# A gated sum of a state-space scan and linear attention: the scan over every sixteenth token instead of every eighth, with a step list drawn up anew

## The chip, the cores and the metric

The kernel runs on one core of one Trainium2 chip. Its five engines work side by side: TensorE (PE in the profile; its weight loads are shown as PEld), VectorE (DVE), ScalarE (ACT), GpSimd (POOL) and SyncE (SP), which here only issues DMAs. The metric is the device time of the slowest core in microseconds; there is only one core. A time is the median of several runs.

## The reference

For x of 2048 tokens and 512 channels (bf16) the output is g * a + (1 - g) * b, with a gate g for each token. Part a is a diagonal complex state-space recurrence with 512 states, part b a linear attention with 32 heads of 16 channels.

```python
g = sigmoid((x * gate_w).sum(-1, keepdims=True))

# a
Lam_bar = exp(dt * Lam)                          # Lam complex, dt = exp(log_dt)
B_bar = ((Lam_bar - 1.0) / Lam)[:, None] * Bmat
Bu = einsum("bld,pd->blp", x + 0j, B_bar)
for t in range(L):
    h = Lam_bar[None, :] * h + Bu[:, t, :]       # hs collects h
a = 2.0 * einsum("blp,dp->bld", hseq, Cmat).real + x * Dskip

# b
phi_q = concat(softmax(q @ w_phi), softmax(-(q @ w_phi)))    # 32 features a head
phi_k = the same of k
kv, z = sum_s phi_k v, sum_s phi_k
b = (phi_q @ kv) / (phi_q @ z + 1e-6) @ wo
```

## The kernel before

**Tokens in residues.** The 2048 tokens are split by their residue r modulo NR = 8. For each r there are NC = 256 columns, two tiles of 128 tokens (index `ti` = 2r + a); the tile pairs lie one after another in `xT`, the transposed x, so that one matmul takes all 256 columns of a residue. Before, column a*128 + c of residue r is token (a*128 + c)*8 + r: a is the half of the sequence. Each x tile is a transposing DMA from HBM (`x_load`), each output tile a DMA into `out_par`.

**The recurrence.** The state dimension is held in eight tiles t of 64 states, real and imaginary part stacked to 128 rows; j = 0 to 3 names a pair of them. Step `g{r}{j}` computes the input products for residue r (eight matmuls of 256 columns against the transposed B, `BT`). For odd r an odd step adds earlier residues: matmuls with `dg`, block-diagonal matrices of the powers 1, 2, 4 and 6 of the decay, against the copies `uv`. So `g7j` ends with the sum of a block of eight tokens, weighted by the decay, for each of 256 blocks, and copies it to `va`, real and imaginary parts separated: four copies of 64 x 256. Step `z{j}` turns this complex recurrence over the 256 blocks into a real one: it multiplies by cosines and sines (`T2c`, `T2s`, tables made by the steps `i{j}` from an iota, two multiplications and two Sin on ScalarE), runs two VectorE scans of length 256 with the decay's eighth power `r8_`, and turns back. The result is the state at the last token of each block, `H7`. The steps `h{r}{j}` then compute the states of residues 0 to 6: a matmul with `dg` against H7 shifted by one block (r = 0, 1, 3, 5), or against the state of r - 1 (r = 2, 4, 6), plus `uv`.

**The rest.** `W`, `f`, `w` fold w_phi into the key and query weights (`W` transposes, `f` and `w` multiply and copy). `k` and `v` are the key and value products of a token tile, `q` the query products; `x`, `n`, `e`, `s` (and for the last groups `X`, `N`, `E`, `S`) are maximum, minimum, exponential and sum of the features, `a` accumulates the key-value matrix. `c` scales C. `y` computes the output products of the recurrence for a token tile, `o` the attention (two matmul groups `pn`, a logarithm, a copy, an exponential, a product, then a transpose by DMA or, for the last four, on TensorE), `t` multiplies with wo into the same PSUM bank, scales by the gate and stores. `M` (on POOL) makes the powers of the decay, `D` (on DVE) spreads them into `dg`. `l`, `N`, `R`, `Q`, `C`, `J`, `O` issue loads on SP: x tiles 8 to 15, the two halves of B (`NI`, `NR`), the transposes of B, of the query weights and of C, copies of the transposed C, and wo.

**What sets the order.** The engines' order is written out by hand, in the string `ORDER` of 865 steps. Each name is a generator that runs up to its next `yield`; the main loop at the end of the function takes the names one by one. A name stands once for each of its yields: `g70 g70` is its matmuls, then the odd step. `@b` gives the PSUM banks that a step may take, `:D` puts a step's PSUM copy or scaling on DVE instead of ScalarE, `:A` issues a store from ScalarE's queue, and `F:n` is n filler matmuls of 128 columns. Each engine takes its instructions strictly in this order. SP too: it runs ahead of the other engines until one of its DMAs has to wait, and what stands behind it waits as well. Ahead of the list SP loads x tiles 0 to 3, the value weights and x tiles 4 to 7.

Of the kernel before, what the change touches and what calls it, by code (L numbers as in the profile page):

```python
# [20 lines left out]
P = 128  # L21
# [13 lines left out]
q0@4 q2 z1 z0 h50@3 z1 z1 g42@7 q0 z1 z1 v10@26 h50 xA z1 h10@0 e4 e4 z1 g42 nA s4 g32@4 v10 g32 a3 g52@3 g32 h60@7 c2
xA s4 c4 O g52 xA c4 R6 z1 z1 v9@26 s4 h10 g52 nA g72@4 g72 c4 h60 v9 a3 J3 g03@3 v11@26 c2 c2 s4 g72 g72 c0 c0 nA
g63@0 z2 z2 v12@74 a3 nA v11 a3 xA g03 z2 z2 z2 z2 xA nA s4 J3 g63 g23@2 c5 s4 v12 g23 h51@6 g13@3 g13 g13 z2 z2 c0 z2
z2 eA g43@0 g43 eA v14@74 v14 J1 h51 s4 g33@2 g33 h52@3 g33 h12@0 g53@6 eA g53 g53 h12 h11@7 h11 h52 eA sA g73@4 g73
g73 g73 v13@26 v13 q10@0 z3 c6 z3 c5 sA z3 z3 v15@73 z3 a4 a4 a4 v15 z3 q10 q5@4 a4 Y z3 h31@0 q5 sA h30@4 z3 q9@2 h31
q13@6 h31 q9 h33@0 h61@7 Y q13 h30 sA sA c5 h62@3 z3 z3 h30 h61 sA Y Y h22@5 q4@2 h62 q4 h33 q15@6 q11@7 h22 h20@4 h20  # L40
h32@2 h32 sA sA c1 q11 h13@1 h13 h32 q14@3 h40@5 h33 c3 h53@7 h42@4 sA h42 h53 c1 c1 sA h21@2 c3 h21 q6@0 q6 q15 c6
q7@1 h63@4 h63 q8@7 h03@0 c3 q7 c6 h40 sA c7 h41@6 h41 y6@2 c7 h03 h03 h43@4 h43 y2@1 h02@5 c7 sA h23@6 h23 h01@0
h00@4 END q8 G X1 y6 y6 q14 y2 N1 X1 h00 h00 N1 y2 h02 h02 X1 N1 G h01 o0@6 y0@7 o0 o0@3 h01 o2@4 o2 X1 o2@5 o2 o2 N1
y5@6 o0 y3@0 X1 N1 y5 X2 o0 o1@4 E1 o2 y0 o2 o0 E1 E1 E1 X2 y1@5 y1 y3 y3 o1 G N2 X2 N2 X2 o0 N2 X2 o3@3 o3 o3@4 S1 o3
o3 G S1 N2 S1 t2 o3 S1 o3 t2 t2:A q12@3 q12 N2 S1 S1 o1@4 o1 o1 o1 o1 S1 S1 E2 S1 y0 y4@1 y9@3 y8@4 y8 y8 X3 E2 E2 S1
S1 S1 N3 X3 E2 t3 X3 X3 X3 S2 N3 t0 t0 t0:A S2 t3 S2 y1 t1 t1 y5 y9 y9 o4@7 o4 o4@0 o4 y4 o4 o4 o4 o5@5 o5 o5@7 o5 o5
y13@0 S2 S2 o6@5 o6 o6@7 o6 o6 y13 N3 y7@5 y7 N3 y7 y13 o5 S2 S2 N3 E3 o5 o6 o6 S2 S2 E3 E3 o7@7 o7:D y4 t4 t4:D t5
o7@7 S2 S2 E3 S3 t5 S2 S3 S3 o7 o7 o7 t6 y11@1 y11 o7 t6 o8@6 o8 o8@7 o8 o8 S3 S3 o8 y12@2 o9@6 o9 o9@7 o8 y11 y12 y12
y10@6 o9 o9 o9 o11@7 o11 o9 S3 S3 y10 y10 o11@7 t7 o11 o11 t7 t8 S3 S3 o11 o11 S3 t8 S3@7 S3:D S3@5 S3 t9 t9 t1:A
o10@4 y15@7 o10:D o10@5 o10:D t8 o10 o10 o10 y15 o12@4 o12:D o12@3 t4 o14@5 o12 o12 o12 t5 o14 t11 o14@4 o14:D o14 o14  # L50
t11 y14@3 t9:A o13@5 o13 o12@4 o12:D y14 o13@1 o13 o13 o15@4 o15:D o15@5 o15 o15 t12 t3:A t10 o13 o13@1 o15 t6:A t11
o14@4 o13:D t7 t10 t10 y15 t12 t12 o15@5 o15 y14 o14:D t13 t14 t14 t14 t13 t13 t15 t15 t15:A
# [18 lines left out]
def kernel(  # L71
# [27 lines left out]
    NC = S // NR  # L99
    NT2 = Pst // 64  # L100
# [7 lines left out]
    out_par = out2.rearrange("(a c r) d -> c r a d", r=NR, c=P)  # L108
# [85 lines left out]
    H7 = pR.tile([P, NT2, ZP + NC], BF16, name="H7")  # L194
# [7 lines left out]
    dg = pBC.tile([P, 4, NT2, P], BF16, name="dg")  # L202
# [18 lines left out]
    T2c = pAC.tile([P, PT, NC], BF16, name="T2c")  # L221
    T2s = pAC.tile([P, PT, NC], BF16, name="T2s")
    uv = [pAC.tile([P, 7, 2, NC], BF16, name=f"uv{j}") for j in range(PT)]
    va = [pAC.tile([P, 2, NC], BF16, name=f"va{j}") for j in range(PT)]
# [4 lines left out]
    x_res = x2.rearrange("(a c r) d -> r a c d", r=NR, c=P)  # L229
# [20 lines left out]
    iot = tabp.tile([P, NC], F32, name="iot", bufs=1)  # L250
    nc.gpsimd.iota(iot[:], pattern=[[1, NC]], base=0, channel_multiplier=0, allow_small_or_imprecise_dtypes=True)
# [15 lines left out]
    dt_, r_, om_, t0, t1, t2, den_, r2_, r4_, om8, r8_ = (par[:, 10 + k, :] for k in range(11))  # L267
# [102 lines left out]
    def st_P4():  # L370
        VS(out=om8, in0=t0, scalar1=float(NR), scalar2=None, op0=ALU.mult)
# [10 lines left out]
    def st_M():  # L382
# [24 lines left out]
        GT(out=dl[:, 9, :], in0=tb[:, 0, :], in1=den_, op=ALU.mult)  # L407
        GT(out=dl[:, 8, :], in0=tb[:, 1, :], in1=den_, op=ALU.mult)
        lo = dl[:, 0:10, :].rearrange("p (k t) j -> p k t j", t=2)
        up = dl[:, 10:20, :].rearrange("p (k t) j -> p k t j", t=2)  # L410
        GS(out=up[:, 0:4, 0], in0=lo[:, 0:4, 1], scalar1=-1.0, scalar2=None, op0=ALU.mult)
        GC(out=up[:, 0:4, 1], in_=lo[:, 0:4, 0])
        GS(out=up[:, 4, 0], in0=lo[:, 4, 0], scalar1=-1.0, scalar2=None, op0=ALU.mult)
        GC(out=up[:, 4, 1], in_=lo[:, 4, 1])
        for h in range(2):
            for ri in range(2):
                GC(out=dgB[ri * 64:(ri + 1) * 64, :, :, h], in_=dl[h * 64:(h + 1) * 64, 10 * ri:10 * ri + 10, :])
        yield

    def st_D():  # L420
# [189 lines left out]
    def st_g(r, j):  # L610
# [12 lines left out]
        if r < 7:  # L623
            evac(uv[j][:, r], pg[:])
            yield
            return
# [238 lines left out]
```

## Time and profile before

| what | value |
|---|---|
| three runs | 156.17, 156.59 and 157.39 us; median 156.59 us |
| the profiled execution | span 153.7 us; 2.9 us below the median of the runs |
| granted TensorE clock | 0.995 mean over the span |
| DMA | 17.03 MB in 48737 packets, mean 111 GB/s |
| HBM | read 2.64 MB, written 2.10 MB |

The span reaches from the first to the last instruction of the program in one profiled execution. The time of a run also has what lies around the span, so the difference of 2.9 us stays in the sum as it is. An engine's busy time counts matmuls, loads of weights and elementwise instructions; a DMA issue, a wait or a branch is not busy time. Matmuls are pipelined, their recorded ends are modelled, and a few matmul records are missing from the trace, so counts of matmuls are taken from the loops of the kernel. A row of the groups reads: line, engine, operation, written tile <- read tiles, shape and type out and in, count | busy us in all, mean ns of one | idle time of the engine just before them, and what ended it.

### The profile page before, as it was taken

To read this page: it belongs to the slowest core of one execution; us is meant where nothing else is said; L and a number is where in the kernel's file an instruction comes from. 1 tells how busy PE (TensorE), PEld (TensorE's weight loads), DVE (VectorE), ACT (ScalarE), POOL (GpSimd) and SP (SyncE) were. 2 spreads that over 40 slices of the span, in tenths; PEclk is the share of its full clock that TensorE was granted. 3 is DMA by queue.
4 is the path that set the end of the run, shared out by engine and by line. 5 is a ranking of instruction groups with operands and counts; after the bars stand their busy time and mean duration, and the time that the engine had idled before them with its cause. 6 is when DMAs were issued, how large, how long until landed. Compare 5 with 4: busy or idle time off the path is not lost.

```text
span 153.7 us, 3412 instructions
## 1 busy us (share of the span) xinstructions
PE 145.5 (95%) x1238; PEld 99.7 (65%) x1254; DVE 131.0 (85%) x302; ACT 136.7 (89%) x322; POOL 12.9 (8%) x43
## 2 busy tenths in 40 slices
PE   7799999999999999999999999999999899999990
PEld 7656665886899858889876565554545455555550
DVE  3599999999999999999999999999999858445510
ACT  3599999999999999999999999999798897577672
POOL 8258800000000000000000000000000000000000
PEclk9999999999999999999999999999999999999998
DMA  4788995544474379960000006603139938667633
GB/s 117 162 220 121 213 171 102 102 86 92 101 102 100 80 146 205 237 133 0 2 4 2 0 0 134 125 18 68 33 82 118 215 80 194 141 118 172 211 123 102
DMA packets 48737, 17.03 MB, mean 111 GB/s; under 512 B 42064, under 2 KB 48720, under 8 KB 48720
## 3 DMA queue, kind: packets, MB, share of 16 engines
q1 hardware_dynamic: 47008, 15.36, 50.6%
q10 hardware_dynamic: 1552, 1.44, 2.9%
q8 instruction: 10, 0.16, 0.5%
q0 software_dynamic: 160, 0.01, 0.2%
q14 instruction: 7, 0.06, 0.1%
HBM read 2.64 MB, written 2.10 MB: 31 GB/s over the span
## 4 chain that ended last, share of the span: by engine, by line
ACT 48%; PE 31%; DMA 8%; DVE 6%; issue 3%; POOL 2%; ACTq 0%; POOLq 0%
PE py L734 12%; ACT EEk L140 12%; ACT uv L121 9%; PE py L782 6%; ACT vx L121 5%; PE pq L478 5%; ACT Xq L121 5%; ACT phT L603 4%; PE ph L685 3%; ACT va L121 3%; DMA phT<-EEq 3%; DMA oT<-on 3%; PE pn L753 2%; DMA vec_n<-in_A_log_dt_dram 2%; ACT EEq L140 2%
## 5 line engine op out<-in xcount | busy, mean ns | idle before, releaser
L614 PE MATMUL pgq<-xT,BT 128*128 128x256 bf16 x256 | 31.5, 272 | 0.0
L614 PEld LDWEIGHTS <-BT 128*128 128x128 bf16 x256 | 24.7, 98 | 3.5
L140 ACT ACTIVATE EEk<-EEk 128x1024 bf16<-128x1024 bf16 x20 | 21.3, 1099 | 0.0
L478 PEld LDWEIGHTS <-xT 128*128 128x128 bf16 x128 | 12.2, 97 | 11.0 <-issue 0.2
L121 ACT CAST uv<-pgq 128x512 bf16<-128x512 f32 x28 | 16.7, 638 | 0.0
L492 PE MATMUL pv<-Wv,xT 128*128 128x256 bf16 (+1 forms) x128 | 16.5, 273 | 0.1
L478 PE MATMUL pq<-Wq,xT 128*128 128x512 bf16 x60 | 15.2, 379 | 0.2
L782 PE MATMUL py<-Wo,oT 128*128 128x512 bf16 x59 | 14.7, 379 | 0.6 <-DMA oT<-on 0.3
L478 PE MATMUL pk<-Wk,xT 128*128 128x512 bf16 x60 | 14.9, 379 | 0.2
L492 PEld LDWEIGHTS <-xT 128*128 128x128 bf16 x128 | 12.5, 98 | 3.1 <-issue 0.2
L786 ACT ACTIVATE ot<-py,G 128x512 bf16<-128x512 f32 x15 | 9.8, 684 | 2.9 <-PE py L782 2.4
L140 ACT ACTIVATE EEq<-EEq 128x1024 bf16<-128x1024 bf16 x12 | 11.8, 1084 | 0.3 <-DVE EEq L535 0.3
L603 ACT ACTIVATE phT<-X,dgB 128x512 bf16<-128x512 bf16 x16 | 11.1, 751 | 0.0
L140 ACT ACTIVATE ld<-pn 128x16 f32<-128x16 f32 x32 | 6.4, 204 | 5.2 <-PE pn L753 5.0
L121 ACT CAST vx<-pv 128x256 bf16<-128x256 f32 x32 | 10.7, 435 | 0.0
L121 ACT CAST nu<-pn 128x256 bf16<-128x256 f32 x26 | 10.0, 400 | 0.0
L556 DVE TENSOR_TENSOR EEk<-EEk,rck 128x4096 bf16<-128x4096 bf16 (+1 forms) x5 | 9.3, 1860 | 0.1
L121 ACT CAST Xq<-pq 128x512 bf16<-128x512 f32 x16 | 9.0, 604 | 0.4 <-PE pn L753 0.4
L782 PEld LDWEIGHTS <-oT 128*128 128x128 bf16 x64 | 5.7, 98 | 5.7 <-DMA oT<-on 0.5
L753 PEld LDWEIGHTS <-phT 128*128 128x128 bf16 x128 | 6.4, 97 | 4.6 <-DMA phT<-EEq 1.3
L761 DVE TENSOR_TENSOR on<-nu,rd 128x512 bf16<-128x512 bf16 x16 | 6.6, 422 | 2.6 <-ACT rd L140 2.1
L519 DVE TENSOR_TENSOR smk<-smk 128x512 bf16<-128x512 bf16 (+4 forms) x18 | 8.1, 449 | 0.1
(179 smaller groups left out, 322.9 us busy)
## 6 DMA issues: line engine op xcount, KB each, us to landing
X<-HM SPq DMA_DIRECT2D x8, 256.0 KB, 4.7
out_dram<-ot SPq DMA_DIRECT2D x9, 128.0 KB, 2.2
out_dram<-ot ACTq DMA_DIRECT2D x7, 128.0 KB, 2.0
C2r<-in_B_wqkv_dram ACTq DMA_DIRECT2D x2, 256.0 KB, 3.5
Wv<-in_B_wqkv_dram SPq DMA_DIRECT2D x1, 512.0 KB, 4.0
Bn<-in_A_B_im_dram SPq DMA_DIRECT2D x1, 512.0 KB, 5.5
Bn<-in_A_B_re_dram SPq DMA_DIRECT2D x1, 512.0 KB, 5.9
Wo<-in_B_wo_dram SPq DMA_DIRECT2D x1, 512.0 KB, 5.9
```

Of the source, the lines that this page charges most:

```text
L121: nc.scalar.copy(out=out_ap, in_=in_ap)
L140: ins = nc.scalar.activation(**kw)
L478: MM(out=pt[:], lhsT=xT[:, kt, ti * P:(ti + 1) * P], rhs=W[:, kt, :], start=(kt == 0), stop=(kt == KT - 1))
L492: MM(out=pv[c][:], lhsT=xT[:, kt, ti * P:(ti + 1) * P], rhs=Wvg[:, kt, c * hd:(c + 1) * hd + c], start=(kt == 0), stop=(kt == KT - 1))
L519: VT(out=dst, in0=cur[:, :, :, 0:n, :], in1=cur[:, :, :, n:2 * n, :], op=op)
L556: VT(out=E5, in0=E5, in1=rc.to_broadcast([P, L, 2 * NB, Dh, 4]), op=ALU.mult)
L603: nc.scalar.mul(out=t_, in_=x_, mul=c_)
L614: MM(out=pg[:, h, :], lhsT=BT[:, kt, 2 * j + h, :], rhs=xT[:, kt, r * NC:(r + 1) * NC], start=(h == 0 and kt == 0), stop=(r % 2 == 0 and k ...
L734: MM(out=py[:], lhsT=hs(r, t, slice(a * P, (a + 1) * P)), rhs=C2B[t], start=(t == 0), stop=False)
L753: MM(out=pn[:, 4 * m:4 * m + 4, :].rearrange("p h e -> p (h e)"), lhsT=ph[:, 4 * hf + m, :], rhs=KVm[:, 4 * hf + m, :], start=(m == 0), st ...
L782: MM(out=py[:], lhsT=oT[:, g, :], rhs=Wo[:, g, :], start=False, stop=(g == HG - 1))
L786: nc.scalar.mul(out=ot[:], in_=py[:], mul=G[:, ti:ti + 1])
```

## The change

A block has sixteen tokens instead of eight. Column a*128 + c of residue r is now token c*16 + a*8 + r: a is the half of a sixteen-token block, and rows of one x or output tile lie 16 tokens apart in HBM instead of 8. After `g7j` the 256 columns of the PSUM tile are the sums of the first half blocks (128 columns) and of the second half blocks (128). A new copy `ua` takes the first halves for all 128 rows; two matmuls of 128 columns with a fifth `dg` matrix, the eighth power of the decay, add them to the second halves in place (the join). The four `va` copies then take 128 columns each. `z` and the tables work on N2 = 128 columns, the scan with the sixteenth power `r16_`. It gives the state at the end of each sixteen-token block, the second half of H7. A new step `Z{j}` (the split) computes the state at the end of the first halves: two matmuls of 128 columns of the same `dg` matrix against H7 shifted by one, and a VectorE sum with `ua` into H7. `M` and `D` make one more power.

```diff
     NC = S // NR
+    N2 = NC // 2
...
-    out_par = out2.rearrange("(a c r) d -> c r a d", r=NR, c=P)
+    out_par = out2.rearrange("(c a r) d -> c r a d", r=NR, c=P)
...
-    H7 = pR.tile([P, NT2, ZP + NC], BF16, name="H7")
+    H7 = pR.tile([P, NT2, ZP + NC + 2], BF16, name="H7")
...
-    dg = pBC.tile([P, 4, NT2, P], BF16, name="dg")
+    dg = pBC.tile([P, 5, NT2, P], BF16, name="dg")
...
-    x_res = x2.rearrange("(a c r) d -> r a c d", r=NR, c=P)
+    x_res = x2.rearrange("(c a r) d -> r a c d", r=NR, c=P)
...
         cmul(6, m2, m4)
+        cmul(8, m4, m4)
...
+        GT(out=r16_, in0=r8_, in1=r8_, op=ALU.mult)
...
             evac(uv[j][:, r], pg[:])
             yield
             return
+        evac(ua[j][:], pg[:, :, 0:N2])
+        yield
+        for h in range(2):
+            MM(out=pg[:, h, N2:NC], lhsT=dg[:, 4, 2 * j + h, :], rhs=ua[j][:, h, :], start=False, stop=True, skip_group_check=True)
+        yield
         for h in range(2):
             for ri in range(2):
-                evac(va[j][h * 64:(h + 1) * 64, ri, :], pg[ri * 64:(ri + 1) * 64, h, :])
+                evac(va[j][h * 64:(h + 1) * 64, ri, :], pg[ri * 64:(ri + 1) * 64, h, N2:NC])
             yield
...
-        rb = r8_[:, j:j + 1].to_broadcast([P, NC])
-        w = sw.tile([P, 2, NC], BF16, name="w")
+        rb = r16_[:, j:j + 1].to_broadcast([P, N2])
+        w = sw.tile([P, 2, N2], BF16, name="w")
...
-                VT(out=H7[ri * 64:(ri + 1) * 64, 2 * j + h, ZP:ZP + NC], in0=mc[hp, ri, :], in1=ms[hp, 1 - ri, :], op=op)
-            yield
+                VT(out=H7[ri * 64:(ri + 1) * 64, 2 * j + h, ZP:ZP + N2], in0=mc[hp, ri, :], in1=ms[hp, 1 - ri, :], op=op)
+            yield
+
+    def st_Z(j):
+        pz = bank([P, 2, N2], F32, "pz")
+        for h in range(2):
+            MM(out=pz[:, h, :], lhsT=dg[:, 4, 2 * j + h, :], rhs=H7[:, 2 * j + h, ZP - 1:ZP - 1 + N2], start=(h == 0), stop=True, skip_group_check=True)
+        yield
+        VT(out=H7[:, 2 * j:2 * j + 2, ZP + N2:ZP + NC], in0=pz[:], in1=ua[j][:], op=ALU.add)
+        yield
...
         if r == 7:
-            return H7[:, t, cols.start + ZP:cols.stop + ZP]
+            if cols is None:
+                return H7[:, t, ZP - 1:ZP + NC + 1].rearrange("p (s c) -> p s c", s=2)[:, :, 0:N2]
+            return H7[:, t, ZP + N2 - cols.start:ZP + NC - cols.start]
```

The list is drawn up anew as a whole, with 881 steps: two more for each of the four `g7j`, two for each `Z{j}`. Nothing else is added or left out, but nearly every place differs, and with it the order on each engine and in SP's queue, the PSUM banks, and which copies run on DVE. Some places of both, old list first (the beginning, the key and value products, the steps around g73, and for the new list Z2 and Z3):

```text
NI l8 l10 F:28 W1@0 W0@1 W0 B W2@2 W2 NR W1:D W3@3 f1@4 f1 W3:D V@5 V U f0@6
...
k7@6 k7 k6@7 ... v4@14 ... v1@03 v1 k10@6 ... v7@70 ... k8@3 v2@14 v6@25 ... k9@7 k12@0
...
g73@4 g73 g73 g73 v13@26 v13 q10@0 z3 c6 z3
```
```text
F:28 W0@3 B W1@0 W0 W1:D W2@6 W2:D W3@4 W3:D f1@0 f1:D l10 NI NR f2@1 f2 l8 f3@4 V@2 V U P P f0@6
...
k6@4 U M k4 n1 l13 x1 n1 k7@6 ... v4@21 v4 k10@4 v3 k10 v7@76 x2 v1@52 v2@41 e0 v7 k9@3 v2 v1 k8@0
...
z2 Z2@3 h51 eA g43@7 Z2 h52@3
...
g73@0 eA h11 v15@67 g73 a4 sA v15 g73 g73 g73:D q10@3
...
z3 c6 Z3@0 h20@4
```

More of the change, by code (lines that the diff above doesn't have):

```diff
@@ L35 @@
[L35 to L39, printed above, removed]
@@ L53 @@
+o13@1 o15@5 o12@4 t1 o12:D t10 o15:D t3 o13 o13 o15@4 o15 o15 t12 o13 o13@4 y14 y15 o14@1 o15 o15@5 t10 o13:D t13 o15
+o14:D t6 t10:A t14 t12:D t12 t8 t14:D t13 t13:A t9:A t15 t15:D t15:A t14
 """
@@ L220 @@
     BT = pAC.tile([P, KT, NT2, P], BF16, name="BT")
-    T2c = pAC.tile([P, PT, NC], BF16, name="T2c")
-    T2s = pAC.tile([P, PT, NC], BF16, name="T2s")
+    T2c = pAC.tile([P, PT, N2], BF16, name="T2c")
+    T2s = pAC.tile([P, PT, N2], BF16, name="T2s")
     uv = [pAC.tile([P, 7, 2, NC], BF16, name=f"uv{j}") for j in range(PT)]
-    va = [pAC.tile([P, 2, NC], BF16, name=f"va{j}") for j in range(PT)]
+    va = [pAC.tile([P, 2, N2], BF16, name=f"va{j}") for j in range(PT)]
+    ua = [pAC.tile([P, 2, N2], BF16, name=f"ua{j}") for j in range(PT)]
     X1 = pAC.tile([P, NT2, D], BF16, name="X1")
@@ L266 @@
     tb = par[:, 4:6, :]
-    dt_, r_, om_, t0, t1, t2, den_, r2_, r4_, om8, r8_ = (par[:, 10 + k, :] for k in range(11))
+    dt_, r_, om_, t0, t1, t2, den_, r2_, r4_, om8, r8_, r16_ = (par[:, 10 + k, :] for k in range(12))
     GT = nc.gpsimd.tensor_tensor
@@ L370, in st_P4 @@
     def st_P4():
-        VS(out=om8, in0=t0, scalar1=float(NR), scalar2=None, op0=ALU.mult)
+        VS(out=om8, in0=t0, scalar1=float(2 * NR), scalar2=None, op0=ALU.mult)
         yield
```

114 lines of the change are left out of this document (59 added, 55 removed).

## The prediction

> **What bounds the kernel now.** I read the page's busy shares and slices first, then the windows, then the chain of waits for the pace of each kind of matmul. Page, parts 1 and 2:
>
> ```profile
> span 153.7 us, 3412 instructions
> ...
> PE 145.5 (95%) x1238; PEld 99.7 (65%) x1254; DVE 131.0 (85%) x302; ACT 136.7 (89%) x322; POOL 12.9 (8%) x43
> ...
> PE   7799999999999999999999999999999899999990
> ...
> DVE  3599999999999999999999999999999858445510
> ACT  3599999999999999999999999999798897577672
> ```
>
> Three engines look full at once, so a share of busy time cannot say which sets the end. The windows (busy time of each engine in a stretch) show two regimes:
>
> ```profile
> 8.00:40.00 32.00, 31.77 (x253) 22.24 (x257) 31.55 (x81) 31.88 (x77) 8.77 (x29) 1.00 0.75 139
> 40.00:100.00 60.00, 59.42 (x542) 45.74 (x544) 59.24 (x124) 59.59 (x126) 0.00 (x0) 1.00 0.43 85
> 100.00:150.00 50.00, 48.50 (x391) 26.51 (x397) 36.35 (x74) 40.90 (x115) 0.00 (x0) 1.00 0.56 120
> ```
>
> Columns: length, then PE, PEld, DVE, ACT, POOL, then the granted clock. Until 100 us PE, DVE and ACT are all full; behind it only PE is. Matmul ends are modelled, so I test PE by its pace. Chain of waits (start, length, what, count), then the timeline's first key matmul and its last entries:
>
> ```profile
> 85.50 0.88 PE ph L685 x8
> 87.64 1.73 PE pq L478 x8
> 98.12 0.22 PE py L739 x4
> 115.15 4.63 DMA phT<-EEq
> 119.83 0.43 PE pn L753 x8
> 140.36 0.38 PE pn L753 x12
> ```
> ```profile
> 8.40 3.62 PE L478 MATMUL pk<-Wk,xT 128*128 128x512 bf16 x15
> ...
> 147.08 2.54 PE L782 MATMUL py<-Wo,oT 128*128 128x512 bf16 x11
> 147.11 0.58 ACT L121 COPY oT<-po 128x512 bf16<-128x512 bf16 x1
> 148.80 1.84 ACT L786 ACTIVATE ot<-py,G 128x512 bf16<-128x512 f32 x3 [1.10 <-PE py L782]
> 150.67 0.34 ACTq L790 DMA_DIRECT2D out_dram<-ot  x1
> ```
>
> Back to back, a 512-column matmul takes 1.73/8 = 0.216 us, a 256-column one 0.88/8 = 0.110, a 128-column one 0.22/4 = 0.055, a 68-column one 0.38/12 = 0.032. From the loops, counted from the first key matmul: 320 of 512 columns (k, q, y, t), 496 of 256 (g, their odd steps, v, h), 116 of 128 and 256 of 68. That is 69.1 + 54.6 + 6.4 + 8.2 = 138.3 us. From 8.40 to 147.08 + 2.54 = 149.62 there are 141.2 us. **TensorE runs at its pace for 98% of that stretch and idles 2.9 us in all.** ACT and DVE are full too, but they are a second bound, not the first: whatever time they get back can buy at most those 2.9 us, plus what lies before 8.40 and behind 149.62.
>
> **The change part by part.** Rows for the elementwise terms (groups by form: busy, mean ns of one):
>
> ```profile
> L654 DVE TENSOR_TENSOR_SCAN w<-ssm_par,ut 128x256 bf16<-128x256 f32 x8 | 5.1, 675 | 0.0
> L641 DVE TENSOR_TENSOR mc<-va,T2c 128x512 bf16<-128x512 bf16 x4 | 1.7, 422 | 0.1
> L519 DVE TENSOR_TENSOR mxk<-mxk 128x256 bf16<-128x256 bf16 x6 | 1.7, 284 | 0.0
> L519 DVE TENSOR_TENSOR mxk<-mxk 128x128 bf16<-128x128 bf16 x6 | 1.3, 218 | 0.0
> L665 DVE TENSOR_TENSOR H<-mc,ms 64x256 bf16<-64x256 bf16 x16 | 4.6, 285 | 0.2
> L447 DVE TENSOR_SCALAR kk<-iot,ssm_par 128x256 f32<-128x256 f32 x4 | 1.6, 444 | 0.0
> L708 DVE TENSOR_TENSOR KVm<-kvacc,maskN 128x256 bf16<-128x256 f32 x2 | 0.8, 410 | 0.0
> L426 DVE TENSOR_TENSOR dg<-idn,phT 128x4096 bf16<-128x4096 bf16 x1 | 2.3, 2292 | 0.0
> L121 ACT CAST va<-pgq 64x256 bf16<-64x256 f32 x16 | 6.0, 372 | 0.1
> L121 ACT CAST nu<-pn 128x256 bf16<-128x256 f32 x26 | 10.0, 400 | 0.0
> L146 ACT ACTIVATE T2c<-kk,hpi_t 128x256 bf16<-128x256 f32 x4 | 2.1, 524 | 0.0
> L786 ACT ACTIVATE ot<-py,G 128x512 bf16<-128x512 f32 x15 | 9.8, 684 | 2.9 <-PE py L782 2.4 <-ACT ot L786 0.4
> L788 DVE TENSOR_SCALAR ot<-py,G 128x512 bf16<-128x512 f32 x1 | 0.7, 742 | 0.0
> ```
>
> *TensorE.* No matmul goes. Each of the four g7 steps gets two 128-column matmuls (join) and each new Z step two more (split): 16 x 0.055 = **+0.9 us**, all on the bound engine. The trace has a row for just this form (py L739, a weight load with each), so 0.9 it is; even at the 256-column pace of 0.110 it would be 1.8, the upper end. "TensorE: Matmul & The Clock Gate" of the Trainium skill, section Back-to-back issue gap, puts a sustained stream of weight load and 128-column matmul at about 81 ns each, which would make it an estimated 1.3; the 55 ns of the row here disagrees, and I keep the row.
>
> *VectorE.* Per j the eight products, sums and writes of z halve. The four mc/ms go from 0.422 to 0.284 (the 256-column row): 16 x 0.14 = 2.2 us off. The two ut go from 0.284 to 0.218: 0.5 off. The H writes of half width, not in the trace, lie between no gain and half of 0.285; by the same fall 0.07 each, 1.1 off. The scans lie between no gain and half of 5.1; 675 ns for 256 elements is dear per element, so I take nearly half, 2.4 off. The tables (kk, psi, abs at 128 columns) give about a third of the 0.444 row, 12 x 0.13 = 1.5 off. Added: four Z sums like the KVm row, 1.6, and a quarter more of dg, 0.6. Net **5.5 us less** DVE work. *ScalarE.* The 16 va copies fall by some 0.09 each (between nothing and half of 0.372), 1.4 off; the eight Sin by some 0.15, 1.2 off; four new ua copies at 0.400, 1.6 on: **1.0 us less**. The new list also hands ScalarE work to DVE: some output scalings (0.684 against 0.742), three products of c, two va pairs, two weight copies. Both engines come out with more slack against TensorE than before.
>
> None of this is on the bound. What it can buy is idle PE time, for instance ahead of the pn at 119.83, which the chain shows released by a phT transpose whose EEq had to come from ScalarE and DVE. I book **-1.2 us** out of the 2.9, somewhat under half, because the rest is spread over many short waits (copies feeding a next matmul, transposes) that no engine's load decides; bounds -2.0 and +0.5.
>
> *M on POOL* gains four small operations; dg needs them at 24.6 us, while POOL ends before 20 us. No cost; if the cover went, they would delay dg by about a microsecond.
>
> ```profile
> 20.00:30.00 10.00, 9.93 (x85) 7.07 (x85) 9.86 (x21) 9.97 (x30) 0.00 (x0) 1.00 0.69 120
> ...
> 24.62 2.29 DVE L426 TENSOR_TENSOR dg<-idn,phT 128x4096 bf16<-128x4096 bf16 x1
> ```
>
> *The list: the loads.* SP issues loads one after another. The new list puts l10 first, then both halves of B, then l8 and l9. For l9 nothing changes: the same transfers stand ahead of it. It is issued at 16.68 and lands 5.7 us later, at 22.4; its reader, k9, starts here at 23.68:
>
> ```profile
> 16.68 1.31 SPq L232 DMA_TRANSPOSE xT<-in_A_x_dram  x1
> ...
> xT<-in_A_x_dram SPq DMA_TRANSPOSE x1, 5.7
> ...
> 23.68 0.38 PE L478 MATMUL pk<-Wk,xT 128*128 128x512 bf16 x1
> ```
>
> In the new list k8 (4 x 0.216) and v6 (8 x 0.110) come behind k9 instead of ahead, so TensorE asks for l9 1.75 us sooner, at 21.9: **+0.5 us** of waiting (0 to 1.0, with the bounds of the landing); PE takes its matmuls in order, so all that stand behind k9 come later by that. Rows of x are now 16 KB apart instead of 8 in each transposing load; no row shows that pitch, so I take nothing, with a few tenths on l9 as the upper end and no reason for a gain. The R and X loads keep their lead: SP stood idle for 28 us before the next transposes it had to issue.
>
> ```profile
> SPq L579 <- DVE HM L689: 28.0, 1, 28.0
> ```
>
> *The list: a new hand-off.* In g7, TensorE waits between the odd step and the join for ScalarE's ua copy. For j = 0, 1, 2 the list puts at least 0.9 us of matmuls in between. For j = 3 it puts only one a step (8 x 0.032 = 0.26) behind the odd step (4 x 0.110), while ScalarE must first do the vx copies of v15 (two at 0.435 overlapping, and a short one), then ua at 0.40: some 1.2 us of work against 0.7 of cover, **+0.5 us** (0 to 0.9). Queued behind that join are the q10 matmuls, so all of PE waits.
>
> ```profile
> L121 ACT CAST vx<-pv 128x256 bf16<-128x256 f32 x32 | 10.7, 435 | 0.0
> ```
>
> *The end.* Behind the last matmul (149.62) ScalarE still has a scaling to finish and starts the last at 149.95. The new list gives t15's and t14's to DVE: the last starts some 0.3 sooner and takes 0.06 longer, **-0.2 us** (+0.2 to -0.4).
>
> Sum against the profiled execution: +0.9 - 1.2 + 0.5 + 0.5 - 0.2 = +0.5, a span of 154.2. Around the span lie 156.59 - 153.7 = 2.9 us to the runs' median, which no part touches: **157.1 us**.
>
> **The rivals.** *A, the slack closes the idle time.* With DVE and ScalarE some microseconds lighter, the two new waits may be covered and 2.0 of the 2.9 us go: 156.6 + 0.9 - 2.0 - 0.2 = 155.3, and 154.6 if l9 also comes early and all but 0.2 us of the idle goes. For it: ACT at 59.59 of 60 us between 40 and 100. Against: waits on DMA landings and on a copy's own length stay.
>
> *B, the split is late.* Z reads H7, which the last of ten DVE steps of z writes; in the list Z2 comes directly behind z2 and Z3 with one ScalarE step between. If DVE is behind at those places, TensorE stands for a write (0.22), and the h behind for a matmul's latency and the sum (0.22 + 0.41): 0.85 each. With both bare and the regained idle halved: 157.1 + 1.7 + 0.6 = 159.4. It decides from the point where DVE's remaining work at Z exceeds TensorE's since the va copies. For it: DVE at 59.24 of 60. Against: z is 1.4 us a j lighter.
>
> *C, TensorE has room after all.* The chain of waits gives ScalarE more of the span than PE:
>
> ```profile
> ACT 48%; PE 31%; DMA 8%; DVE 6%; issue 3%; POOL 2%; ACTq 0%; POOLq 0%
> ```
>
> If the two elementwise engines set the end, their 6.5 us, halved by sharing, come through: 156.6 - 3.2 - 0.2 = 153.2. "Perfetto Trace Analysis" of the Trainium skill, section Identifying the Most-Contended Engine, would have headroom judged by weight-load share and FLOP share rather than matmul busy time; the 65% of weight loads alone points to C. Against it stands the pace sum, 98%.
>
> **How the numbers follow.** Forecast 0.57, A 0.17, B 0.21, C 0.05. The forecast's five terms lie apart in the kernel, so I add the distances to their bounds as squares: down 0.8, 0.5, 0.5 and 0.2, together 1.1; up 0.9, 1.7, 0.5, 0.4 and 0.4, together 2.1; its own range is 156.0 to 159.2. Taking in A's 155.3 and about half of B, the range is 155.1 to 159.3. About 1% (1.6 us) is what a measurement of this kernel can tell from no change. Faster by more (under 155.0): all of C and a third of A, 0.10. Slower by more (over 158.2): B's 0.21 and 0.09 of the forecast, its top, 0.30. Within: 0.60.
>
> **What would show it.** Right: 16 more 128-column matmuls at 0.055; k9 starting when its load lands, about 22.4; a gap ahead of the last join; short last scaling on DVE; longer idle stretches on DVE and ACT between 40 and 100 us. Wrong: TensorE idle well under 1.5 us (A), gaps ahead of Z or the h behind it (B), matmuls at a slower pace with half-width operands, or a span shortened by over 3 us (C).

## The result, and the profile after

| | before | after |
|---|---|---|
| median (range) | 156.5 us (156.17 to 157.39) | 162.46 us (161.70 to 162.98) |
| ratio, 95% interval | | 1.0378 [1.0332, 1.0423] |
| profiled execution, span | 153.7 us | 161.0 us |

The changed kernel is 5.9 us slower, above the top of the predicted range. The two profiled executions lie further apart, 7.3 us, because after's is the longest of its four (162.98) and before's is a short one: a run of either kernel lasts about 2.0 us longer than its own span, so 0.9 of the 2.9 us that were taken as lying around the span is the difference between this execution and the median run.

The page of after, parts 1, 2 and 4:

```profile
span 161.0 us, 3464 instructions
...
PE 148.8 (92%) x1254; PEld 101.3 (63%) x1270; DVE 135.5 (84%) x322; ACT 133.1 (83%) x313; POOL 12.9 (8%) x47
...
PE   7899889499999999999999999989999979889990
...
DVE  3899997687799999899999999999799958845552
ACT  3599999979999998999999999959799794544750
...
PEclk9999999969999999999999999999999999999999
...
PE 40%; DVE 33%; ACT 12%; DMA 10%; issue 2%; DVEq 0%; ACTq 0%
```

Before, TensorE's row read 9 from the third slice on, with a single 8, to the last but one. Now the fifth to eighth slices (16 to 32 us) read 8, 8, 9, 4, and the ninth has a clock digit of 6; some late slices read 7 and 8. The chain of waits names TensorE first now, with VectorE at 33%: it says which work released the next, not how much an engine was delayed.

The windows of after (length, PE, PEld, DVE, ACT, POOL, then the granted clock):

```profile
8.00:40.00 32.00, 28.79 (x197) 19.14 (x199) 27.46 (x77) 30.22 (x71) 8.79 (x33) 0.95 0.73 138
40.00:100.00 60.00, 59.72 (x571) 47.19 (x573) 56.92 (x129) 58.20 (x123) 0.00 (x0) 1.00 0.34 69
100.00:158.00 58.00, 53.91 (x425) 29.65 (x431) 46.31 (x91) 41.27 (x115) 0.00 (x0) 1.00 0.59 123
...
30.00:40.00 10.00, 8.96 (x71) 6.97 (x72) 8.65 (x18) 8.67 (x21) 0.00 (x0) 0.83 0.55 89
...
33.00:34.00 1.00, 1.00 (x7) 0.70 (x5) 0.89 (x1) 1.00 (x4) 0.00 (x0) 0.50 0.84 132
```

The middle stage, which holds the scans, joins and splits, has lost nothing: TensorE busy 59.72 of 60 us, more than before, with VectorE and ScalarE slacker. The loss lies ahead of 40 us (28.79 busy of 32, before 31.77) and behind 100 us. By the prediction's pace the matmuls are 138.3 + 0.9 = 139.2 us of work; from the first key matmul (7.87) to the last end (157.27) there are 149.4. TensorE's idle time, with the time at a low clock, has grown from 2.9 to 10.2 us: that is the whole difference of the spans (+7.3 of idle time, +0.9 of matmuls, a start 0.5 earlier and an end 0.4 shorter).

What happens ahead of 40 us? First TensorE, then ScalarE, both in the timeline of after (start, length, what; in brackets the idle time before it and what released it):

```profile
22.53 2.76 PE L483 MATMUL pk<-Wk,xT 128*128 128x512 bf16 x12 [0.44 <-DMA xT<-in_A_x_dram]
...
29.99 1.03 PE L619 MATMUL pgq<-xT,BT 128*128 128x256 bf16 x8 [1.18 <-ACT Xq L123]
32.01 1.06 PE L599 MATMUL kvacc<-vx,EEk 128*128 128x68 bf16 x16 [0.99 <-ACT gl L501]
32.99 1.87 PE L497 MATMUL pv<-Wv,xT 128*128 128x256 bf16 x8
34.66 1.38 PE L619 MATMUL pgq<-xT,BT 128*128 128x256 bf16 x8
35.88 0.38 PE L624 MATMUL pgq<-uv,dg 128*128 128x256 bf16 x2
```
```profile
16.05 1.28 ACT L142 ACT_TABLE_LOAD   x1
17.34 1.06 ACT L142 ACTIVATE EEk<-EEk 128x1024 bf16<-128x1024 bf16 x1
...
26.24 1.28 ACT L142 ACT_TABLE_LOAD   x1
27.53 0.31 ACT L142 ACTIVATE lgk<-smk 128x128 f32<-128x128 f32 x1
27.86 1.28 ACT L142 ACT_TABLE_LOAD   x1
29.16 0.31 ACT L142 ACTIVATE rck<-lgk 128x128 bf16<-128x128 f32 x1
29.37 0.57 ACT L123 CAST Xq<-pk 128x512 bf16<-128x512 f32 x1
29.95 1.28 ACT L134 ACT_TABLE_LOAD   x1
```

The load of k9 behaves as predicted: its matmul starts at 22.53. The two waits at 29.99 and 32.01 are for ScalarE's copies, and ScalarE was loading function tables: 1.28 us each, at 26.24 for a logarithm, at 27.86 for an exponential, at 29.95 once more. The kernel before shows the same two functions with no load between them:

```profile
25.20 0.49 ACT L140 ACTIVATE lgk<-smk 128x128 f32<-128x128 f32 x1
25.72 0.31 ACT L140 ACTIVATE rck<-lgk 128x128 bf16<-128x128 f32 x1
```

The timeline of before has three table loads in the whole execution (1.89, 9.09, 17.59 us), that of after six. The third of before comes from `pin_act_set` in the step `L`, which preloads one set that serves exponential and logarithm. The old list has `R1 L e0`: L ahead of the first exponential. The new list has `e0` and `s0` (among whose yields are a logarithm and an exponential) ahead of `L`: `s0 s0 s0 x2 D v6@45 g40@2 k9 L`. Without the preload each function gets a load of its own at line 142, and L loads the common set only then. "ScalarE: Activation LUTs" of the Trainium skill, section Table sets, states that one set holds both exponential and logarithm, so that the two share one load. The trace of before agrees: behind the load at 17.59 it has no other.

### The profile page after: what moved, and what is told of

Its sections match the earlier page's. It is cut to its first block, busy times and chain, and to the rows that moved or that the text cites. A ratio compares the mean times of both kernels' runs of the same rounds, so it can differ in the third digit from the quotient of the medians.

```text
span 161.0 us, 3464 instructions
## 1 busy us (share of the span) xinstructions
PE 148.8 (92%) x1254; PEld 101.3 (63%) x1270; DVE 135.5 (84%) x322; ACT 133.1 (83%) x313; POOL 12.9 (8%) x47
## 4 chain that ended last, share of the span: by engine, by line
PE 40%; DVE 33%; ACT 12%; DMA 10%; issue 2%; DVEq 0%; ACTq 0%
PE py L754 9%; PE pgq L619 8%; PE py L802 7%; PE pv L497 4%; DVE smk L524 4%; DMA phT<-EEq 3%; DMA phT<-EEk 3%; DVE EEk L561 3%; ACT vx L123 2%; ACT EEk L142 2%; DMA oT<-on 2%; DVE Bn L709 2%; DMA C2r<-in_B_wqkv_dram 2%; DVE mnk L524 2%; DVE mxk L524 2%
## 5 line engine op out<-in xcount | busy, mean ns | idle before, releaser
L619 PE MATMUL pgq<-xT,BT 128*128 128x256 bf16 x256 | 32.7, 274 | 1.2 <-ACT Xq L123 1.2
L497 PE MATMUL pv<-Wv,xT 128*128 128x256 bf16 (+1 forms) x128 | 17.2, 282 | 0.3 <-ACT gl L501 0.2
L123 ACT CAST uv<-pgq 128x512 bf16<-128x512 f32 x28 | 16.2, 621 | 1.0 <-PE pgq L624 0.4
L802 PE MATMUL py<-Wo,oT 128*128 128x512 bf16 x61 | 15.3, 379 | 1.0 <-DMA oT<-on 0.9
L808 DVE TENSOR_SCALAR ot<-py,G 128x512 bf16<-128x512 f32 x9 | 6.7, 748 | 5.7 <-PE py L802 5.6
L773 PE MATMUL pn<-KVm,phT 128*128 128x68 bf16 x128 | 7.8, 194 | 1.9 <-DMA phT<-EEq 1.2
L608 ACT ACTIVATE phT<-X,dgB 128x512 bf16<-128x512 bf16 x13 | 9.4, 753 | 0.0
L123 ACT CAST Xq<-pk 128x512 bf16<-128x512 f32 x15 | 8.5, 605 | 0.0
```

The costliest lines, as they stand in the source:

```text
L123: nc.scalar.copy(out=out_ap, in_=in_ap)
L497: MM(out=pv[c][:], lhsT=xT[:, kt, ti * P:(ti + 1) * P], rhs=Wvg[:, kt, c * hd:(c + 1) * hd + c], start=(kt == 0), stop=(kt == KT - 1))
L608: nc.scalar.mul(out=t_, in_=x_, mul=c_)
L619: MM(out=pg[:, h, :], lhsT=BT[:, kt, 2 * j + h, :], rhs=xT[:, kt, r * NC:(r + 1) * NC], start=(h == 0 and kt == 0), stop=(r % 2 == 0 and k ...
L773: MM(out=pn[:, 4 * m:4 * m + 4, :].rearrange("p h e -> p (h e)"), lhsT=ph[:, 4 * hf + m, :], rhs=KVm[:, 4 * hf + m, :], start=(m == 0), st ...
L802: MM(out=py[:], lhsT=oT[:, g, :], rhs=Wo[:, g, :], start=False, stop=(g == HG - 1))
```

## The experiments

A difference of two ratios is turned into time with 156.5 us; all ratios are against the kernel before on the same chip.

### The table preload

**e1_table_early**: the changed kernel with L moved.

```diff
- n1 x1 k6:D x1 i1 e0 k7 ...  D v6@45 g40@2 k9 L v6
+ n1 x1 k6:D x1 i1 L e0 k7 ...  D v6@45 g40@2 k9 v6
```

> The changed kernel with one step of its list moved: L, which pins ScalarE's table set, goes ahead of the first exponentials e0 (as in the old list) instead of behind the first logarithm. Theory (late L): three table loads of 1.28 us go (16.05, 26.24, 27.86 in the changed trace become one), TensorE's waits at 28.4 and 30.8 and its half clock from 33 to 35 go with them; 162.5 falls to 157 to 158.5. Rival 1 (the new joins, splits and matmuls cost it): no more than 1 us goes, 161.5 or above. Rival 2 (the rest of the list, late waits for transposes): about half goes, 159 to 160.5, and the waits at 106, 130 and 140 us stay.

**e2_table_late**: the kernel before with L moved the other way.

```diff
- R1 L e0 n1 ... k11@1 s0 e1 M k11
+ R1 e0 n1 ... k11@1 s0 e1 L M k11
```

> The kernel before with L moved behind the first logarithm and the reciprocal's exponential, nothing else. Theory (late L): three more table loads, 3.8 us more on ScalarE before 35 us, which was full; 156.5 rises by 3 to 5 us, to 159.5 to 161.5. Rivals 1 and 2: the place of L costs what its loads hide behind, under 1 us, 156.5 to 157.5.

Measured: e1 159.09 us, 1.0172 [1.0155, 1.0190], 3.2 us less than after by the ratios. e2 160.63 us, 1.0267 [1.0240, 1.0293], 4.2 us more than before. TensorE's timeline of e1:

```profile
23.50 2.76 PE L483 MATMUL pk<-Wk,xT 128*128 128x512 bf16 x12 [1.19 <-DMA xT<-in_A_x_dram]
...
30.50 0.67 PE L599 MATMUL kvacc<-vx,EEk 128*128 128x68 bf16 x16
...
32.77 0.38 PE L624 MATMUL pgq<-uv,dg 128*128 128x256 bf16 x2
...
101.76 0.30 PE L773 MATMUL pn<-KVm,phT 128*128 128x68 bf16 x4
103.83 0.56 PE L773 MATMUL pn<-KVm,phT 128*128 128x68 bf16 x12 [0.47 <-DMA phT<-EEk]
127.36 1.04 PE L802 MATMUL py<-Wo,oT 128*128 128x512 bf16 x4 [0.57 <-DMA oT<-on]
137.80 0.30 PE L773 MATMUL pn<-KVm,phT 128*128 128x68 bf16 x4 [0.95 <-DMA phT<-EEq]
```

Both waits for copies are gone, and so is something else. From the kvacc matmuls to the odd step behind them (line 624) are 2.27 us here and 3.87 in after (32.01 to 35.88) for the same matmuls: in after these ran at half clock (0.50 in the window from 33 to 34 us), behind two stalls in a row. So in the profiled execution the loads cost TensorE some 2.5 us of waits (by its pace; the brackets count from the modelled ends) and 1.6 us at half clock; 1.0 of this is lost again in e1, whose k9 starts that much later. The half clock isn't in every execution of after: two of the four have a mean granted clock of 0.989 (162.84 and 162.98 us), two of 1.000 (161.70 and 162.08). At 1.000 the loads cost 2.9 us against the two executions of e1 at 1.000 (158.92 and 159.00), and the half clock comes to some 1.0 us more. e2 shows the same signature in the old list. The same window of e2:

```profile
30.00:40.00 10.00, 8.36 (x81) 6.66 (x82) 7.54 (x16) 9.41 (x20) 0.00 (x0) 0.83 0.56 93
```

The late preload is shown from both sides: taken from the one, put into the other. (L also closes the buffers of the tables and opens those of the scan, so that these move with it in both.) e2 fell into its theory's range. e1 did not: 159.09 lies above the 157 to 158.5 of its theory and in the range of its rival 2, and the waits for transposes stayed, as that rival says. So e1 leaves 2.7 us that the preload doesn't explain. The next experiments look for them.

### The new scan in the old list, the old scan in the new

**e3_old_list**: the changed scan, but the old list with the new steps put in (`g7j` joins and `Z{j}`, eight places) and q3, v13 and h50 moved a few places beside them, L early as there. Two of the places:

```diff
- z1 z0 h50@3 z1 z1 g42@7 q0 z1 z1
+ z1 z0 Z0@0 z1 Z0 z1 g42@7 q0 h50@3 z1 z1
...
- z3 z3 h30 h61 sA Y Y
+ z3 z3 Z3@6 h30 h61 Z3 sA Y Y
```

> The changed scan in the old list: only the twelve splits and joins are put in (two steps for each g7, two for each Z), nothing else moves, L stays early. Theory (late L): the scan itself costs its 16 matmuls, 0.9 us, and a few short waits, against some idle time won; 156 to 158. Rival 1 (joins and splits): 160 or above. Rival 2 (the list): like the theory, 156 to 158.

**e10_old_scan**: the kernel before with the list of e1, the 16 new steps taken out.

> The new list with L ahead of e0, but the old computation: 8-token blocks, scan over 256 blocks, no joins and no splits (their 16 steps are taken out of the list). It tells the list from the scan. Against the first experiment (159.1 us) it lacks 16 matmuls of 128 columns, 0.9 us, and gives VectorE and ScalarE back the work that the change took off. If the rest of the loss is the new list's (late loads, late transposes), it stays when the scan goes: 158 to 159. If the rest is the scan's joins and splits, the time is the kernel before's: 156 to 157. If the new list only holds because the scan is lighter, VectorE is late at z and the time is above 159.5.

Measured: e3 164.16 us, 1.0499 [1.0477, 1.0521]; e10 165.93 us, 1.0576 [1.0539, 1.0612]. e3 went to its rival 1, joins and splits (160 or above), and e10 to its third case (above 159.5); its trace shows TensorE waiting 1.6 us for a VectorE sum of an h step, not VectorE late at z. The waits of e3 (who waits on whom: total, times, longest):

```profile
DVE mc L651 <- ACT va L123: 4.2, 3, 1.7
DVE H L683 <- PE pz L681: 3.9, 4, 2.2
...
PE pz L681 <- ACT Xq L123: 1.9, 2, 1.2
PE pz L681 <- DVE H L675: 1.6, 1, 1.6
```

Here TensorE stands at the splits (line 681), for a PSUM bank that a copy must free and for VectorE's last write of H7: what the prediction's rival B describes. These waits make 3.5 of the 7.8 us that e3 loses; the rest is not taken apart. In the changed kernel's waits neither appears. Each list fits its own scan only: the new list with the old scan loses 6.3 us against e1, the old list with the new scan loses 7.8 against before. e3 also shows the sizes of the changed operations (groups by form: busy, mean ns of one):

```profile
L123 ACT CAST va<-pgq 64x128 bf16<-64x128 f32 x16 | 4.2, 260 | 3.1 <-PE pgq L635 3.0
L675 DVE TENSOR_TENSOR H<-mc,ms 64x128 bf16<-64x128 bf16 x16 | 3.5, 220 | 0.2
L664 DVE TENSOR_TENSOR_SCAN w<-ssm_par,ut 128x128 bf16<-128x128 f32 x8 | 2.9, 410 | 0.0
...
L683 DVE TENSOR_TENSOR H<-pz,ua 128x256 bf16<-128x256 f32 x4 | 1.7, 424 | 3.9 <-PE pz L681 3.9
...
L452 DVE TENSOR_SCALAR kk<-iot,ssm_par 128x128 f32<-128x128 f32 x4 | 1.4, 385 | 0.0
...
L651 DVE TENSOR_TENSOR mc<-va,T2c 128x256 bf16<-128x256 bf16 x4 | 1.2, 291 | 4.2 <-ACT va L123 4.2
```

Halving the columns takes 13% (kk) to 39% (the scan) off an operation here, not 50. VectorE's busy time in e3 is 127.2 us, 3.8 less than before.

### Single terms of the prediction

**e4_pitch**: the kernel before with only the token order of the new one, so that part a is not the reference's.

```diff
-    x_res = x2.rearrange("(a c r) d -> r a c d", r=NR, c=P)
+    x_res = x2.rearrange("(c a r) d -> r a c d", r=NR, c=P)
```

> The kernel before with the token order of the changed one alone: rows of the x and output tiles lie 16 KB apart in HBM instead of 8. The scan then runs over tokens in another order, so a is not the reference's. All theories: 156.5, within 0.5; if the pitch has part in the 5.9 us, the x loads of the first 25 us land later than 4.0 us (median) and the time rises by more.

156.33 us, 0.9993 [0.9974, 1.0012]: the wider pitch of the x and output rows costs nothing (to 0.2 us by the interval). The x loads land after 4.1 us in the median, 4.0 before.

**e9_more_matmuls**: the kernel before with 16 matmuls of 128 columns more.

```diff
+            if r == 7:
+                for h in range(2):
+                    MM(out=pg[:, h, P:NC], lhsT=dg[:, 3, 2 * j + h, :], rhs=uv[j][:, 6, h, 0:P], start=False, stop=True, skip_group_check=True)
...
+            if r == 0:
+                MM(out=ph[:, h, P:NC], lhsT=dg[:, 3, t, :], rhs=uv[j][:, 6, h, 0:P], start=False, stop=True, skip_group_check=True)
```

> The kernel before with 16 more matmuls of 128 columns and nothing else: two in each g7 step, behind the odd step, and two in each h0 step, on operands that are there already (they add wrong terms to the blocks' sums and to the states of residue 0). No copy, no wait and no place in the list is new. Theory, TensorE is the bound and takes 0.055 us for each: +0.9 us, 157.3 against 156.4 (ratio 1.0055, between 1.003 and 1.008). Rival, TensorE has room: the idle time takes them up, ratio 1.000 to 1.002. If each cost the 0.110 us of a 256-column matmul, 158.2 (1.011).

156.98 us, 1.0018 [0.9996, 1.0040]: +0.3 us (-0.1 to +0.6), in the rival's range and below the 0.9 of the theory. With 2.9 us or more of idle time in the kernel, added matmuls can come out of that; where they did, no trace shows.

### Waits taken away by moving steps

Three edits of e1's list, each aimed at one of the waits that its timeline shows, and all three together.

```diff
e5_loads
- l10 NI NR l8 l9 l12 l11 R0 R3 R1
+ l10 l9 NI l8 NR l12 l11 R0 R1 R3
e6_scalings
- t5:D t6:D t7:D t8:D t9:D t12:D t14:D t15:D
+ t5 t6 t7 t8 t9 t12 t14 t15
e7_features
- q14@0 sA h20 h32 q15@4 h61 h33@5 q6 h32 h53
+ q14@0 sA h20 h32 q15@4 sA h61 sA h33@5 q6 h32 sA h53
```

> The kernel of e1_table_early (159.1) with SP's first loads in another order: l10 l9 NI l8 NR instead of l10 NI NR l8 l9, and R1 ahead of R3. In e1 TensorE stood 1.35 us at 22.0 for l9 and 0.7 in two pieces before it. Theory (l9 waits behind both halves of B): l9 lands near 17, the 1.35 us go, B's second half lands a microsecond later and costs at most 0.3 at the first g; 157.6 to 158.1. Rival (ScalarE's copies would hold TensorE there anyway): 158.8 to 159.3, with the wait moved to a copy.

> The kernel of e1_table_early with the output scalings of t5 to t9, t12, t14 and t15 back on ScalarE; the list is otherwise the same. In e1 VectorE stands 4.7 us at the head of its queue for these scalings' matmuls, with feature work queued behind, and ScalarE waits 10 us for pn. Theory (these scalings hold up the features, so the transposes land late): the waits of TensorE at 126 and 137 (0.7 and 1.1 us) shrink by half or more; 157.8 to 158.6. Rival (the features are late since 80 us, from the order of the h sums): 159 or a little more, waits unchanged.

> The kernel of e1_table_early with three steps of sA (the difference, the exponential, the product with it) a few steps earlier in the list, ahead of eight h and c sums of VectorE. Theory (the transposes of sA start at 96.8 us here, at 91.5 in the kernel before, so the first pn matmuls wait 0.3 and 0.6 at 101 and 103): these two waits go; 158.1 to 158.6. Rival (the h sums that now come later are waited for instead): 159 or above.

> The edits of e5, e6 and e7 together on e1. If the three gains are apart from each other they add up: 1.2 + 0.8 + 0.7 off 159.1, 156 to 157.2, close to the kernel before or slightly over it by the 16 matmuls (0.9 us). If TensorE's idle time only moves from one wait to the next: 157.5 to 158.5.

Measured: e5 160.58 us, 1.0248 [1.0193, 1.0304]; e6 161.15 us, 1.0283 [1.0235, 1.0332]; e7 160.41 us, 1.0225 [1.0180, 1.0270]; e8 163.89 us, 1.0487 [1.0428, 1.0546]. None is faster than e1's 1.0172 [1.0155, 1.0190], e5 and e6 are slower, and e8 is the slowest of all. The waits aimed at went in e5 and e7 and hardly changed in e6; in each, others came. From the waits of e5, e6 and e7, in this order:

```profile
PE pgq L635 <- ACT ua L123: 1.5, 1, 1.5
```
```profile
PE pht L579 <- ACT nu L123: 0.7, 1, 0.7
```
```profile
PE ph L705 <- DVE HM L709: 1.1, 1, 1.1
...
PE pq L483 <- DVE Wv L709: 0.6, 1, 0.6
```

In e5 TensorE stands at a join whose `ua` isn't copied yet; in e7 it waits for VectorE's sums of h (line 709), which the earlier features put off, as the rival said. Moving a step mends one place and breaks another, so these runs couldn't tell whether a wait is a loss or only where the loss shows.

**e11_k8_first**: e1's list with k8 and k9 exchanged.

```diff
- v7 k9@3 v2 v1 k8@0 n2
+ v7 k8@0 v2 v1 k9@3 n2
```

> The kernel of the first experiment with k8 and k9 exchanged in the list: the four matmuls of k8 (0.86 us) run while the load l9 is on its way; the loads themselves stay. Theory, TensorE's time standing for l9 (1.35 us there) is lost time: 0.86 of it is covered, 159.1 - 0.9 = 158.2 (157.9 to 158.5). Rival, as with the earlier loads, the wait goes here and comes back at a later place where another engine is as late: 159.0 or more.

158.76 us, 1.0134 [1.0098, 1.0170]: 0.6 us less than e1, and the intervals overlap. The wait of 1.35 us (by TensorE's pace; 1.19 in the bracket) turned into two of 0.44 (k8's own load) and 0.38. Between the theories, and small.

### Waits taken away with other data

A wait can be taken away without moving anything: the instruction reads a tile that is there already.

```diff
e12_other_x: k9 reads x tile 0
-        tile_mm(pk, ti, Wk2)
+        tile_mm(pk, 0 if ti == 9 else ti, Wk2)
e13_no_transposes, on e1; e15_before_no_transposes, on the kernel before
-        ph = phT0[:, n] if n < 4 else live["ph", n // 4][:, n % 4]
+        ph = phT0[:, n % 4]
...
-            MM(out=py[:], lhsT=oT[:, g, :], rhs=Wo[:, g, :], start=False, stop=(g == HG - 1))
+            MM(out=py[:], lhsT=xT[:, g, ti * P:(ti + 1) * P], rhs=Wo[:, g, :], start=False, stop=(g == HG - 1))
e16_no_first: e13, and o0 to o3 read a tile of ones
-                MM(out=pn[:, 4 * m:4 * m + 4, :].rearrange("p h e -> p (h e)"), lhsT=ph[:, 4 * hf + m, :],
+                MM(out=pn[:, 4 * m:4 * m + 4, :].rearrange("p h e -> p (h e)"), lhsT=fillw[:] if n < 4 else ph[:, 4 * hf + m, :],
```

> The kernel of the first experiment, but k9 multiplies x tile 0, which has long been there, instead of tile 9 (so the attention uses wrong keys for one tile); list, loads and every other instruction stay. Theory, TensorE's 1.35 us of standing for l9 are lost time: most of it goes, the next load l8 coming just in time, 159.1 - 1.2 = 157.9 (157.6 to 158.2). Rival, the wait only moves, to k8's or k11's loads or to ScalarE and VectorE, which are as late: 158.7 to 159.2.

> The kernel of the first experiment, but o4 to o15 read the four transposed feature tiles of o0 to o3, and every t reads a tile of x instead of its transposed oT (wrong values; the transposes are still issued, nothing waits for them). Theory, the waits of 0.73 us at 126 and 1.11 us at 137 are lost time and nothing is late behind them: 159.1 - 1.8 = 157.3 (157.0 to 157.7). Rival, the output scalings on VectorE and ScalarE or the logarithms are as late, and TensorE then waits for a free PSUM bank: 158.6 to 159.2.

> Both of the last two edits at once. Theory, the losses lie apart in the kernel and add up: 159.1 - 1.2 - 1.8 = 156.1 (155.7 to 156.7), about the time of the kernel before, though its own waits for transposes (0.52 and 0.50 us) are not taken away. Rival, behind both waits another engine is as late: 158.0 to 159.0.

> The kernel before with the edit of the transposes: o4 to o15 read the transposed features of o0 to o3, every t a tile of x (wrong values; the transposes are still issued, nothing waits for them). Theory, the old list loses only its own two waits of 0.52 and 0.50 us: 156.6 - 1.0 = 155.6 (ratio 0.993 to 0.997), so that about 1 of the 2 us is new in the new list. Rival, its waits are covered by what ScalarE still has to do behind them: 156.2 to 156.6 (0.998 to 1.000), and all of the 2 us are new. If it gains 2 us too (0.988 or less), the transposes explain nothing of the difference.

> As the run without transposes in the new list, and o0 to o3 too read a constant tile of ones in place of their transposed features. Theory, the waits of 0.28 and 0.67 us at 101 and 103 us are lost time: 157.5 - 0.9 = 156.6 (156.3 to 156.9, ratio 0.998 to 1.001). Rival, VectorE, which makes these features, is late for the output scalings just the same, and the waits only move: 157.3 to 157.7 (1.003 to 1.006).

| run | us | ratio to before, 95% | change |
|---|---|---|---|
| e12 (k9 not waiting) | 158.95 | 1.0138 [1.0102, 1.0175] | -0.5 against e1 |
| e13 (later transposes) | 157.51 | 1.0042 [1.0018, 1.0067] | -2.0 against e1 |
| e14 (both) | 157.31 | 1.0046 [1.0024, 1.0068] | +0.1 against e13 |
| e16 (all transposes) | 156.46 | 0.9986 [0.9966, 1.0006] | -0.9 against e13 |
| e15 (later ones, in before) | 155.54 | 0.9922 [0.9905, 0.9940] | -1.2 against before |

The wait for l9, the most visible one of e1, is worth about 0.5 us (e12, -1.2 to +0.1) or nothing (e14 against e13, -0.5 to +0.6). The rival has the other engines as late behind it; that isn't shown, for in e12's trace no new wait takes its place. Nor is such a wait the new list's alone: the profile of e15, with the old list, has one of 1.28 us for a load of x at 20.20 that the profile of before hasn't. The waits for transposes are lost time in full: 2.0 us for the later ones (the theory had 1.8) and 0.9 for the first, as expected, 2.9 in all, each within some 0.5. The price is that of everything a transposed tile needs, for with other data its reader waits for none of it. The kernel before loses 1.2 us of this kind too, and its profile shows no wait for the first ones, so 1.7 us (1.2 to 2.2) are new. e15 against e16 leaves 0.0064, 1.0 us (0.6 to 1.4), for the 16 matmuls (0.3 by e9) and what remains of the load's wait and others.

Why the transposes come later is seen in the timelines of before and of e1, SP's issue of the first features and, in before, the first matmul that reads them:

```profile
91.47 7.43 SPq L579 DMA_TRANSPOSE phT<-EEk  x4
...
100.13 0.29 PE L753 MATMUL pn<-KVm,phT 128*128 128x68 bf16 x4
```
```profile
96.83 6.35 SPq L584 DMA_TRANSPOSE phT<-EEk  x4
```

Before, 8.7 us lie between them; in e1 it is 101.76 - 96.83 = 4.9 us, with the transposes landing 3 to 5 us after their issue: no lead is left. The new list has the features' last steps later among the matmuls. e7 put them back and paid for it elsewhere; no list here has both, and no version of the changed scan that computes the same output beats the kernel before. For the later transposes the leads were not compared.

## Why the prediction was wrong, step by step

**The step that failed** is the reading of the list for ScalarE. The prediction booked **1.0 us less** work there and "more slack against TensorE than before"; it read the new list for its loads, its hand-offs and the engines of its copies, but put the place of `L` at nothing, without a reason. `L` behind the first exponentials adds three table loads, 3.84 us of ScalarE's time, and within 5 us (26.24 to 31.23) there stand three loads where before has none. That is 3.2 of the 5.9 us (2.5 to 4.0 by the intervals). Over the whole span ScalarE did get its slack, 133.1 us busy after 136.7 with the loads in it; a sum over the span doesn't show that TensorE waits for its copies in one stretch. The timeline of before had what was needed: table loads at 1.89, 9.09 and 17.59 us, and the code puts the last under `L`.

**-1.2 us of idle time won back** failed too. In the middle stage it came in part (TensorE 59.42 to 59.72 of 60 us, 0.3), but the prediction let one size hold for the whole kernel. Behind 100 us the waits are for transposes: they grew by 1.7 us. For the first features the later issue shows it (4.9 us of lead after 8.7); that place in the list and not an engine's load sets the later ones too is inferred, from e6 among others, where eight scalings went back to ScalarE and these waits hardly changed. The prediction named one such wait (119.83) as a candidate for gain and never compared the lead in both lists.

**The sum so corrected**, by the ratios: 3.2 (preload) + 1.7 (transposes) + 1.0 (matmuls and the rest) = 5.9 us. The first two are measured; the last is what is left, so that the sum comes out by construction.

**VectorE, 5.5 us less**: 3.8 in e3. The scans were sized well (2.1 us off by e3's row, predicted 2.4), the tables too high (kk takes 0.385 us after 0.444, a seventh less and not a third). And in after itself VectorE is busier than before, 135.5 against 131.0, for the list moves work to it; the largest part shows in the groups of after, where one scaling has become nine:

```profile
L808 DVE TENSOR_SCALAR ot<-py,G 128x512 bf16<-128x512 f32 x9 | 6.7, 748 | 5.7 <-PE py L802 5.6
```

The prediction named these moves but didn't subtract them.

**The 16 matmuls, +0.9**: the pace was right (the two of the join below start at 84.91, the next matmul at 85.02), the size too high; e9 gives 0.3 (to 0.6). "On the bound" wasn't strict with 2.9 us idle.

**k9 and l9, +0.5**: the mechanism was right to a tenth (22.4 predicted, 22.53 measured; in e1, where the loads came later, 23.50), the price at most that: 0.5 or none by e12 and e14.

**The join of g73, +0.5**: no wait there in after, because the list was misread. The excerpt ahead of the prediction lacks one `g73`; the list has `g73@0 g73 eA h11 v15@67 g73 a4 sA v15 g73 g73 g73:D`. So the odd step comes ahead of v15's matmuls, the `ua` copy ahead of v15's copies, and eight v matmuls and eight of a4, 1.15 us, cover it:

```profile
83.65 0.27 PE L626 MATMUL pgq<-uv,dg 128*128 128x256 bf16 x1
83.76 1.05 PE L497 MATMUL pv<-Wv,xT 128*128 128x256 bf16 x8
84.65 0.42 PE L599 MATMUL kvacc<-vx,EEk 128*128 128x68 bf16 x8
84.91 0.27 PE L635 MATMUL pgq<-ua,dg 128*128 128x128 bf16 x2
85.02 1.03 PE L483 MATMUL pq<-Wq,xT 128*128 128x512 bf16 x3
```

**x pitch, nothing**: right (e4). **M on POOL, nothing**: POOL's busy time stayed at 12.9 us, and no wait on it appears. **The end, -0.2**: 157.27 to 161.0 is 3.7 us, before 4.1, so -0.4.

**The rivals.** A and C are out: idle time grew. B's mechanism exists, as e3 shows at several microseconds, but this list covers its splits: of the 0.30 for "slower", B's share pointed at a cause that after doesn't have, and the time came out on that side by other ways. The range's top at 159.3 held e1 (159.09) and not after; without the late L the time lies inside the range, but on its slow side, and with the -1.2 and the join wrong.

## What to carry to other kernels

When an order of work is drawn up anew, check first the rare steps that set a state for later instructions, such as a table preload: one step out of 881 made over half of this loss, and it shows in a profile as instructions that weren't there before. Price a wait by giving its reader other data, not by moving steps: the most visible wait was worth about 0.5 us or nothing, while the smaller late ones were worth their full length. For work that goes out by a transfer and comes back, compare the lead between issue and reader in both orders. And read a wait off the whole order: one step missing from an excerpt gave a wait that wasn't there.

## What the hardware showed

In the profiled execution of after TensorE stood for 1.18 and 0.99 us with eight matmuls between; then the granted clock read 0.50 (33 to 34 us; 0.83 in the window from 30 to 40), and 256-column matmuls ran 0.21 us apart instead of 0.11. A mean of 0.83 over 10 us is 3.4 us at 0.50. In e2, with stalls of 1.02 and 1.28 us at nearly the same place, it came again, with the same 0.83. A single stall of 1.19 us (e1, at 23.50) wasn't followed by it: e1's clock reads 1.00 from 20 to 40 us. That the two stalls set it off is likely, not shown: two of after's four executions have a mean clock of 1.000. Where it came it added about 1 us to the run, and no row of waits shows it; only the clock column does.

A table load takes 1.28 us each time, and the next function starts 0.01 to 0.02 us later. "ScalarE: Activation LUTs" of the Trainium skill, section What ACT_TABLE_LOAD costs, gives 1283 ns for the load and some 1380 ns more for a drain, 2.66 us for a switch. The load agrees; the drain doesn't show in these timelines. e2, with three loads more, takes 4.2 us longer, waits and half clock together.
